# PSUM tiles, buffers and a masked copy in the second half of a two-block attention kernel

## The chip, the cores and the metric

The kernel runs on one core of one Trainium2 chip. The metric is device time in microseconds (us), the slowest core's, here the only one's. Every run is quoted by the median of its executions. "Granted clock" below is the share of full speed at which TensorE's clock was let through, and an "eviction" is a copy out of PSUM, the memory that the matmuls of this kernel write.

## The reference, cut to what matters

Two independent blocks with the same shapes (2048 tokens, width 640, 32 heads of 20) are computed and joined along the last axis. Block A is softmax attention in a sliding window of 256. Block B is linear attention:

```python
phi = lambda t: jnp.where(t > 0, t + 1, jnp.exp(t)) + 1e-6
pq, pk = phi(q), phi(k)
kv  = jnp.einsum("bhsd,bhse->bhde", pk, v)          # 20x20 state per head
z   = jnp.einsum("bhsd->bhd", pk)
num = jnp.einsum("bhqd,bhde->bhqe", pq, kv)
den = jnp.einsum("bhqd,bhd->bhq", pq, z)[..., None] + 1e-6
o   = num / den                                     # then  o @ wo
```

Both blocks end with a 640x640 output projection, called the tail here.

## The kernel before

Order of work: load A; project q, k, v of A; attention of A; then the part that the change touches. That part is, in program order: tail A; the q projection of B with phi; the k and v projections of B with phi; the state `kv_ps` (with a column of ones in v, so that it holds z too); a block-diagonal copy `kvBD` of the state; q times state and the division; tail B. A scheduler orders the instructions of each engine at build time, so work of neighbouring steps interleaves where tiles are free.

The q projection in channel-major form. One PSUM tile holds 128x2048 f32 (`P` by `NQT` times `NQ`), and B has one buffer for it:

```python
for c in range(KT):                                   # 5 channel blocks
    ps = psq.tile([P, NQT, NQ], F32, name="ps")       # psum_bufs=1 for B
    for nt in range(NQT):
        for kt in range(KT):
            nc.tensor.matmul(ps[:, nt, :], ...)       # 20 matmuls of 512 columns
    chunk = stage.tile([P, S], BF16, name="chunk")
    e = scr.tile([P, NQT, NQ], BF16, name="e")
    nc.scalar.activation(out=e[:], in_=ps[:], func=ACT.Exp)
    r = scr.tile([P, NQT, NQ], BF16, name="r")
    nc.scalar.activation(out=r[:], in_=ps[:], func=ACT.Relu)
    ...                                               # min/add on VectorE into chunk
    for h, src_row, cnt, dst_off in head_pieces(c):   # DMA rows into pq_pad[0..7]
        eng.dma_start(out=dst, in_=chunk[src_row : src_row + cnt, :])
```

The tail (both blocks; one buffer for `T2`, one for `pso`):

```python
for tb in range(NT):                                  # 16 token blocks
    T2 = pt2.tile([P, KT, P], BF16, name="T2")
    ...                                               # 5 transposes
    oT = tsb.tile([P, KT, P], BF16, name="oT_cmp")
    nc.any.tensor_copy(out=oT[:], in_=T2[:])
    pso = pto.tile([P, 1024], F32, name="pso")
    ...                                               # 10 matmuls
    osb = tsb.tile([P, D], BF16, name="osb")
    nc.any.tensor_copy(out=osb[:], in_=pso[:, 0:D])
    nc.sync.dma_start(out=out2[...], in_=osb[:])
```

The state and its block-diagonal copy, and the first use of it:

```python
nc.any.memset(kvBD[:], 0.0)
...                                                   # 8 groups x 16 matmuls into kv_ps
for hg in range(HG):
    for j in range(4):                                # 32 copies of 20x21
        nc.any.tensor_copy(
            out=kvBD[HD * j : HD * j + Dh, hg, HD * j : HD * j + HV],
            in_=kv_ps[HD * j : HD * j + Dh, hg % 2, hg // 2, HV * j : HV * j + HV],
        )
...
for tb in range(NT):
    O_ps = psn.tile([P, HG, P], F32, name="O_psB")
    for hg in range(HG):
        nc.tensor.matmul(O_ps[:, hg, :], lhsT=pq_pad[hg][:, tb * P : (tb + 1) * P],
                         rhs=kvBD[:, hg, :], start=True, stop=True)
    ...                                               # den, reciprocal, multiply -> otokB
```

The softmax here doesn't subtract the row's maximum and nothing guards it: scores larger than these inputs give would overflow.

Of the kernel before, what the change touches and what calls it, by code (L numbers as in the profile page):

```python
# [8 lines left out]
P = 128  # L9
ALU = mybir.AluOpType  # L10
ACT = mybir.ActivationFunctionType
BF16 = mybir.dt.bfloat16
F32 = mybir.dt.float32
# [3 lines left out]
def kernel(  # L17
# [40 lines left out]
    while h0 < H:  # L58
# [26 lines left out]
        base=-1,  # L85
        channel_multiplier=1,
    )
    woA_sb = const.tile([P, KT, D], BF16, name="woA_sb")
    woB_sb = const.tile([P, KT, D], BF16, name="woB_sb")
    otokA = const.tile([P, NT, D], BF16, name="otokA")  # L90
# [16 lines left out]
    dma_engines = [nc.sync, nc.scalar, nc.gpsimd]  # L107

    def proj_channel_major(
        name, xT, w, col_base, pads, mode, psum_bufs, stage_bufs, sbuf_side="right"  # L110
    ):
        with ExitStack() as stack:
            psq = stack.enter_context(
                tc.tile_pool(name=f"psq_{name}", bufs=psum_bufs, space=bass.MemoryType.PSUM, side="left")
            )
            stage = stack.enter_context(
                tc.tile_pool(name=f"stage_{name}", bufs=stage_bufs, side=sbuf_side)
            )
            scr = None
            if mode == "phi":  # L120
                scr = stack.enter_context(
                    tc.tile_pool(name=f"scr_{name}", bufs=1, side=sbuf_side)
                )
            dcount = 0
            for c in range(KT):
                ps = psq.tile([P, NQT, NQ], F32, name="ps")
                for nt in range(NQT):
                    for kt in range(KT):
                        nc.tensor.matmul(  # L129
                            ps[:, nt, :],  # L130
                            lhsT=w[:, kt, col_base + c * P : col_base + (c + 1) * P],
                            rhs=xT[:, kt, nt * NQ : (nt + 1) * NQ],
                            start=(kt == 0),
                            stop=(kt == KT - 1),
                        )
                chunk = stage.tile([P, S], BF16, name="chunk")
                cv = chunk[:].rearrange("p (n f) -> p n f", f=NQ)
                if mode == "scale":
                    nc.scalar.activation(out=cv, in_=ps[:], func=ACT.Copy, scale=scale)  # L139
                elif mode == "copy":  # L140
                    nc.any.tensor_copy(out=cv, in_=ps[:])  # L141
                elif mode == "phi":
                    e = scr.tile([P, NQT, NQ], BF16, name="e")
                    nc.scalar.activation(out=e[:], in_=ps[:], func=ACT.Exp)
                    r = scr.tile([P, NQT, NQ], BF16, name="r")
                    nc.scalar.activation(out=r[:], in_=ps[:], func=ACT.Relu)  # L146
                    nc.vector.tensor_scalar(
                        out=cv,
                        in0=e[:],
                        scalar1=1e-6,  # L150
                        scalar2=1.0 + 1e-6,
                        op0=ALU.add,
                        op1=ALU.min,
                    )
                    nc.vector.tensor_tensor(out=cv, in0=cv, in1=r[:], op=ALU.add)
                else:
                    raise ValueError(mode)
                for h, src_row, cnt, dst_off in head_pieces(c):
                    hg, j = divmod(h, 4)
                    dst = pads[hg][HD * j + dst_off : HD * j + dst_off + cnt, :]  # L160
                    eng = dma_engines[dcount % len(dma_engines)]
                    dcount += 1
                    eng.dma_start(out=dst, in_=chunk[src_row : src_row + cnt, :])

    def proj_token_major(name, xT, w, col_base, dstv_fn, mode, psum_bufs):
        with ExitStack() as stack:
# [38 lines left out]
                else:  # L205
                    raise ValueError(mode)

    def tail(name, o_tok_all, wo_sb, col0, stack, psum_side, psum_bufs):
        if True:
            pt2 = stack.enter_context(  # L210
                tc.tile_pool(name=f"pt2_{name}", bufs=psum_bufs, space=bass.MemoryType.PSUM, side=psum_side)
            )
            pto = stack.enter_context(
                tc.tile_pool(name=f"pto_{name}", bufs=psum_bufs, space=bass.MemoryType.PSUM, side=psum_side)
            )
            tsb = stack.enter_context(tc.tile_pool(name=f"tsb_{name}", bufs=2, side="right"))
            for tb in range(NT):
                T2 = pt2.tile([P, KT, P], BF16, name="T2")
                for c in range(KT):
                    nc.tensor.transpose(  # L220
                        T2[:, c, :], o_tok_all[:, tb, c * P : (c + 1) * P], ident[:]
# [4 lines that stand above are left out]
                for c in range(KT):  # L226
                    for n0 in range(0, D, NQ):
                        n1 = min(D, n0 + NQ)
                        nc.tensor.matmul(  # L229
                            pso[:, n0:n1],  # L230
                            lhsT=oT[:, c, :],
                            rhs=wo_sb[:, c, n0:n1],
                            start=(c == 0),
                            stop=(c == KT - 1),
                        )
                osb = tsb.tile([P, D], BF16, name="osb")
                nc.any.tensor_copy(out=osb[:], in_=pso[:, 0:D])  # L237
                nc.sync.dma_start(
                    out=out2[tb * P : (tb + 1) * P, col0 : col0 + D], in_=osb[:]
                )  # L240
# [11 lines left out]
    vaugA_v = vaugA[:].rearrange("p t (h e) -> p t h e", e=HV)  # L252
    nc.vector.memset(vaugA_v[:, :, :, Dh:HV], 1.0)

    proj_channel_major("qA", xTA, wA, 0, q_pad, "scale", psum_bufs=2, stage_bufs=5)
    proj_channel_major("kA", xTA, wA, D, k_pad, "copy", psum_bufs=2, stage_bufs=5)
    proj_token_major(
        "vA", xTA, wA, 2 * D, lambda tb: vaugA_v[:, tb, :, 0:Dh], "copy", psum_bufs=2
    )
# [80 lines left out]
    for g in range(HG):  # L340
# [10 lines left out]

    tstA = ExitStack()
    tail("A", otokA, woA_sb, 0, tstA, "right", 1)
    proj_channel_major(
        "pqB", xTB, wB, 0, pq_pad, "phi", psum_bufs=1, stage_bufs=4, sbuf_side="left"
    )
    tstA.close()

    with ExitStack() as stack:
        pst = stack.enter_context(  # L360
            tc.tile_pool(name="pst_kvB", bufs=2, space=bass.MemoryType.PSUM, side="left")
        )
        scrt = stack.enter_context(tc.tile_pool(name="scrt_kvB", bufs=2, side="right"))
        for tb in range(NT):
            ps = pst.tile([P, 1536], F32, name="pstkv")
            for n0 in range(0, 2 * D, NQ):
                n1 = min(2 * D, n0 + NQ)
# [26 lines left out]

    kvsb = ctx.enter_context(tc.tile_pool(name="kvsb", bufs=1, side="right"))
    kvBD = kvsb.tile([P, HG, P], BF16, name="kvBD")
    nc.any.memset(kvBD[:], 0.0)
    with ExitStack() as kvs:
        kvp = kvs.enter_context(tc.tile_pool(name="kvp", bufs=1, space=bass.MemoryType.PSUM, side="left"))
        kv_ps = kvp.tile([P, 2, 4, P], F32, name="kv_ps")  # L400
        for hg in range(HG):
            for tb in range(NT):
                nc.tensor.matmul(  # L403
                    kv_ps[:, hg % 2, hg // 2, 0 : 4 * HV],
                    lhsT=pk_pad[:, tb, hg * P : (hg + 1) * P],
                    rhs=vaugB[:, tb, hg * 4 * HV : (hg + 1) * 4 * HV],
                    start=(tb == 0),
                    stop=(tb == NT - 1),
                )
        for hg in range(HG):  # L410
            for j in range(4):
                nc.any.tensor_copy(  # L412
                    out=kvBD[HD * j : HD * j + Dh, hg, HD * j : HD * j + HV],
                    in_=kv_ps[HD * j : HD * j + Dh, hg % 2, hg // 2, HV * j : HV * j + HV],
                )
    stB2.close()

    persB3 = ctx.enter_context(tc.tile_pool(name="persB3", bufs=1, side="left"))
    otokB = persB3.tile([P, NT, D], BF16, name="otokB")
    with ExitStack() as nms:  # L420
        psn = nms.enter_context(tc.tile_pool(name="psn", bufs=2, space=bass.MemoryType.PSUM, side="left"))
        nrmB = nms.enter_context(tc.tile_pool(name="nrmB", bufs=2, side="left"))
        for tb in range(NT):
            O_ps = psn.tile([P, HG, P], F32, name="O_psB")
            for hg in range(HG):
                nc.tensor.matmul(  # L426
                    O_ps[:, hg, :],
                    lhsT=pq_pad[hg][:, tb * P : (tb + 1) * P],
                    rhs=kvBD[:, hg, :],
                    start=True,  # L430
                    stop=True,
                )
            ov = O_ps[:].rearrange("p g (j e) -> p g j e", e=HD)
            den = nrmB.tile([P, HG, 4, 1], F32, name="denB")
            nc.vector.tensor_scalar_add(out=den[:], in0=ov[:, :, :, Dh : Dh + 1], scalar1=1e-6)  # L435
            recip = nrmB.tile([P, HG, 4, 1], F32, name="recipB")
# [5 lines left out]
                in1=recip[:].to_broadcast([P, HG, 4, Dh]),  # L442
                op=ALU.mult,
            )
        tail("B", otokB, woB_sb, D, nms, "right", 1)


# [28 lines left out]
```

## Time and profile before

465.16 us, median of 6 runs (463.51 to 466.59).

| stretch before, us | what | TensorE busy | what the rest is |
|---|---|---|---|
| 0 to 286.7 | block A up to its attention | 246.3 | not touched by the change |
| 286.7 to 336.5 | tail A with part of the q projection of B | 44.0 of 49.8 | waits for evictions |
| 336.5 to 353.6 | rest of the q projection of B | 9.5 of 17.1 | two waits for Exp and Relu |
| 353.6 to 397.1 | k and v projections of B | 43.2 of 43.5 | dense |
| 397.1 to 412.5 | state and its copies | 6.6 of 15.4 | TensorE waits |
| 412.5 to 438.4 | q times state, division, half of tail B | 24.0 of 25.9 | VectorE 22.0 |
| 438.4 to 463.9 | nine blocks of tail B | 15.9 of 25.5 | waits for copies |

The table by windows of the profile before. The columns after the window and its length are busy time (with the number of instructions) of the engines, the mean granted TensorE clock, the share of the DMA engines and GB/s:

```profile
core 0: us, PE busy (x) PEld busy (x) DVE busy (x) ACT busy (x) POOL busy (x), PEclk, DMA share, GB/s
286.70:336.50 49.80, 44.04 (x302) 23.11 (x307) 23.31 (x32) 21.24 (x22) 8.72 (x8) 0.97 0.27 78
336.50:353.60 17.10, 9.52 (x31) 3.57 (x31) 2.63 (x4) 7.98 (x5) 0.99 (x2) 0.80 0.18 53
353.60:397.06 43.46, 43.16 (x235) 23.38 (x239) 13.53 (x31) 29.91 (x45) 1.51 (x3) 1.00 0.05 13
397.06:412.50 15.44, 6.58 (x129) 6.56 (x129) 0.91 (x2) 7.43 (x35) 0.95 (x1) 0.80 0.01 2
412.50:438.40 25.90, 24.00 (x234) 16.62 (x238) 21.96 (x54) 5.36 (x8) 0.00 (x0) 0.86 0.12 39
438.40:463.90 25.50, 15.91 (x128) 9.12 (x130) 3.98 (x9) 7.00 (x11) 0.00 (x0) 1.00 0.19 65
```

From 412.5 to 438.4 the profile shows TensorE 24.00 us at matmuls and 16.62 us at weight loads in 25.90 us, so the two overlap, and it shows the ends of matmuls as modelled; 24.0 of 25.9 therefore does not show that matmuls bound that stretch. What does is seen instruction by instruction. The timeline of the kernel before (start, duration, engine, line, operation, output and inputs, count; in brackets the idle time of the engine before it and what ended it), first around the q projection of B:

```profile
338.89 1.88 ACT L144 ACTIVATE e<-ps 128x2048 bf16<-128x2048 f32 x1 [0.39 <-PE ps L129]
340.67 1.87 ACT L146 ACTIVATE r<-ps 128x2048 bf16<-128x2048 f32 x1
342.59 7.21 PE L129 MATMUL ps<-xT_inB,w_inB 128*128 128x512 bf16 x20 [3.73 <-ACT r L146]
353.60 6.65 PE L369 MATMUL pstkv<-w_inB,xT_inB 128*128 128x512 bf16 x34 [3.79 <-ACT r L146]
```

One PSUM tile, one buffer: TensorE stands 3.73 us until Exp and Relu have read it. The twenty matmuls behind it take 7.21 us, 0.36 us each, where packed matmuls of this shape, such as the ten before the wait, start 0.216 us apart. The granted clock was 0.50 from 342.6 to 347.

Next, the timeline around the state:

```profile
399.14 6.56 PE L403 MATMUL kv_ps<-vaugB,pk_pad 128*128 128x84 bf16 x128 [2.11 <-ACT vaugB L392]
405.81 6.42 ACT L412 CAST kvBD<-kv_ps 20x21 bf16<-20x21 f32 x32 [6.72 <-PE kv_ps L403]
412.48 2.81 PE L426 MATMUL O_psB<-kvBD,pq_pad 128*128 128x128 bf16 x16 [6.79 <-ACT kvBD L412]
```

Thirty-two tiny copies take 6.42 us of ScalarE in a row, 0.20 us each for 420 numbers, and TensorE waits 6.79 us for them. And in the last stretch, two steps of tail B:

```profile
443.54 0.49 DVE L224 COPY oT_cmp<-T 128x640 bf16<-128x640 bf16 x1 [1.97 <-PE T L220]
444.09 1.53 PE L229 MATMUL pso<-woB_sb,oT_cmp 128*128 128x512 bf16 x9 [0.65 <-DVE oT_cmp L224]
446.49 1.53 PE L229 MATMUL pso<-woB_sb,oT_cmp 128*128 128x512 bf16 x10 [0.58 <-DVE oT_cmp L224]
```

Each block of 2.40 us has a hole near 0.6 us in which TensorE waits for its transposed input to be copied out of the only transpose buffer.

### The profile page before, as it was taken

Reading aid. Unit: us, or ns where it says so; the run is one execution under the profiler, and the core shown is the slowest. Engines: PE = TensorE matmul, PEld = TensorE weight load, DVE = VectorE, ACT = ScalarE, POOL = GpSimd, SP = SyncE. Lnnn points to the kernel's source line nnn. Section 1 sums busy time; section 2 is a strip of 40 time slices with the busy share of each in tenths; the row PEclk is TensorE's granted clock in tenths of the full one; section 3 lists DMA queues with packets and bytes.
Section 4 is the critical chain, followed back from the end, with each engine's and each line's share of the span. In section 5 each row is a group of like instructions: output and inputs, shape, how many; then the busy total and the mean of one; then the engine's idle time right before and its main releaser. Section 6 shows DMA issues by size and latency. Waiting matters only on the chain. (4 is left out here: it accounts for less than half of the span.)

```text
span 463.9 us, 10081 instructions
## 1 busy us (share of the span) xinstructions
PE 389.5 (84%) x4291; PEld 225.8 (49%) x4316; DVE 195.0 (42%) x497; ACT 274.7 (59%) x322; POOL 25.8 (6%) x48
## 2 busy tenths in 40 slices
PE   0498979889999999999999999889866999739875
PEld 0143435455555555655555555445423555626642
DVE  0000251066656665565665656624412332128721
ACT  1034103589888899899888886651435777342222
POOL 1013120000000000000000002200101000000000
PEclk9999999965555555555555555999979999868999
DMA  8954341095000000000000000033321000001111
GB/s 178 316 152 120 95 127 47 12 232 199 3 1 1 4 2 1 3 1 1 4 2 1 3 1 1 30 95 111 96 76 52 1 0 1 1 1 44 58 62 66
DMA packets 34361, 25.56 MB, mean 55 GB/s; under 512 B 23180, under 2 KB 32396, under 8 KB 34316
## 3 DMA queue, kind: packets, MB, share of 16 engines
q1 hardware_dynamic: 31628, 19.65, 15.0%
q0 software_dynamic: 1632, 2.61, 2.4%
q10 hardware_dynamic: 1056, 2.66, 2.3%
q8 instruction: 34, 0.56, 0.5%
q14 instruction: 11, 0.09, 0.1%
HBM read 6.55 MB, written 5.24 MB: 25 GB/s over the span
## 5 line engine op out<-in xcount | busy, mean ns | idle before, releaser
L297 ACT ACTIVATE p<-S_ps 128x1152 bf16<-128x1152 f32 (+3 forms) x176 | 173.5, 1041 | 20.4 <-PE S_ps L288 16.2
L288 PE MATMUL S_ps<-q_pad,k_pad 20*128 20x128 bf16 x1440 | 117.1, 289 | 15.6 <-ACT p L297 13.7
L317 PE MATMUL O_qb<-vaugA,p 128*128 128x21 bf16 x1440 | 96.1, 185 | 1.7 <-DVE p L307 0.9
L317 PEld LDWEIGHTS <-p 128*128 128x128 bf16 x1440 | 64.4, 106 | 55.9 <-DVE p L301 26.9
L301 DVE TENSOR_TENSOR p<-p,maskE 128x384 bf16<-128x384 bf16 (+1 forms) x154 | 53.9, 350 | 57.8 <-ACT p L297 56.8
L307 DVE TENSOR_TENSOR p<-p,maskD 128x384 bf16<-128x384 bf16 (+1 forms) x176 | 60.6, 345 | 24.8 <-ACT p L297 24.2
L129 PE MATMUL ps<-xT_inA,w_inA 128*128 128x512 bf16 x196 | 45.8, 397 | 20.3 <-DMA w_inA<-in_A_wqkv_dram 18.0
L288 PEld LDWEIGHTS <-k_pad 20*128 20x128 bf16 x1440 | 46.4, 104 | 29.4 <-issue 18.8
L237 ACT CAST osb<-pso 128x640 bf16<-128x640 f32 x25 | 17.4, 694 | 51.8 <-PE pso L229 39.1
L369 PE MATMUL pstkv<-w_inB,xT_inB 128*128 128x512 bf16 (+1 forms) x235 | 43.2, 343 | 4.1 <-ACT r L146 3.8
L129 PEld LDWEIGHTS <-w_inA 128*128 128x128 bf16 x200 | 20.2, 101 | 45.7 <-DMA w_inA<-in_A_wqkv_dram 18.0
L229 PEld LDWEIGHTS <-oT_cmp 128*128 128x128 bf16 x320 | 24.1, 98 | 34.9 <-DVE oT_cmp L224 12.0
L369 PEld LDWEIGHTS <-xT_inB 128*128 128x128 bf16 x240 | 23.5, 98 | 24.0 <-issue 3.6
L141 DVE CAST chunk<-ps 128x2048 bf16<-128x2048 f32 x4 | 9.2, 2291 | 56.3 <-PE ps L129 54.3
L129 PE MATMUL ps<-xT_inB,w_inB 128*128 128x512 bf16 x96 | 28.7, 437 | 4.1 <-ACT r L146 3.7
L229 PE MATMUL pso<-woB_sb,oT_cmp 128*128 128x128 bf16 (+1 forms) x154 | 25.5, 301 | 6.7 <-DVE oT_cmp L224 4.7
L139 ACT ACTIVATE chunk<-ps 128x2048 bf16<-128x2048 f32 x5 | 9.4, 1877 | 33.1 <-PE ps L129 30.7
L229 PE MATMUL pso<-woA_sb,oT_cmp 128*128 128x128 bf16 (+1 forms) x157 | 24.3, 298 | 5.4 <-ACT oT_cmp L224 2.9
L190 ACT CAST vaugA<-pst 128x640 bf16<-128x640 f32 x14 | 9.7, 695 | 29.1 <-PE pst L180 29.1
L180 PE MATMUL pst<-w_inA,xT_inA 128*128 128x128 bf16 (+1 forms) x157 | 21.7, 297 | 2.8 <-DVE chunk L141 2.6
L224 DVE COPY oT_cmp<-T 128x640 bf16<-128x640 bf16 x22 | 10.7, 489 | 20.5 <-PE T L220 20.3
L378 ACT ACTIVATE et<-pstkv 128x640 bf16<-128x640 f32 x16 | 11.3, 704 | 13.1 <-PE pstkv L369 13.1
(47 smaller groups left out, 243.8 us busy)
## 6 DMA issues: line engine op xcount, KB each, us to landing
out_dram<-osb SPq DMA_DIRECT2D x32, 160.0 KB
w_inA<-in_A_wqkv_dram SPq DMA_DIRECT2D x3, 800.0 KB
w_inB<-in_B_wqkv_dram SPq DMA_DIRECT2D x3, 800.0 KB
woA_sb<-in_A_wo_dram SPq DMA_DIRECT2D x1, 800.0 KB
woB_sb<-in_B_wo_dram SPq DMA_DIRECT2D x1, 800.0 KB
q_pad<-chunk SPq DMA_DIRECT2D x10, 80.0 KB
q_pad<-chunk POOLq DMA_DIRECT2D x10, 80.0 KB, 3.6
k_pad<-chunk SPq DMA_DIRECT2D x10, 80.0 KB
```

The source lines that it names most:

```text
L129: nc.tensor.matmul(ps[:, nt, :], lhsT=w[:, kt, col_base + c * P : col_base + (c + 1) * P], rhs=xT[:, kt, nt * NQ : (nt + 1) * NQ], start=( ...
L180: nc.tensor.matmul(ps[:, n0:n1], lhsT=xT[:, kt, tb * P : (tb + 1) * P], rhs=w[:, kt, col_base + n0 : col_base + n1], start=(kt == 0), stop ...
L224: nc.any.tensor_copy(out=oT[:], in_=T2[:])
L229: nc.tensor.matmul(pso[:, n0:n1], lhsT=oT[:, c, :], rhs=wo_sb[:, c, n0:n1], start=(c == 0), stop=(c == KT - 1),)
L237: nc.any.tensor_copy(out=osb[:], in_=pso[:, 0:D])
L288: nc.tensor.matmul(S_ps[:, i, kbi, :], lhsT=k_pad[hg][HD * j : HD * j + Dh, kb * P : (kb + 1) * P], rhs=q_pad[hg][HD * j : HD * j + Dh, qb ...
L297: nc.scalar.activation(out=p[:, 0:nh, 0:nkb, :], in_=S_ps[:, 0:nh, 0:nkb, :], func=ACT.Exp)
L301: nc.vector.tensor_tensor(out=p[:, 0:nh, 0, :], in0=p[:, 0:nh, 0, :], in1=maskE[:, None, :].to_broadcast([P, nh, P]), op=ALU.mult,)
L307: nc.vector.tensor_tensor(out=p[:, 0:nh, nkb - 1, :], in0=p[:, 0:nh, nkb - 1, :], in1=maskD[:, None, :].to_broadcast([P, nh, P]), op=ALU.mult,
L317: nc.tensor.matmul(O_qb[:, oslot(h), 0:HV], lhsT=p[:, i, kbi, :], rhs=vaugA[:, kb, h * HV : (h + 1) * HV], start=(kbi == 0), stop=(kbi == ...
L369: nc.tensor.matmul(ps[:, n0:n1], lhsT=xTB[:, kt, tb * P : (tb + 1) * P], rhs=wB[:, kt, D + n0 : D + n1], start=(kt == 0), stop=(kt == KT - 1),
L378: nc.scalar.activation(out=e[:], in_=kv_view, func=ACT.Exp)
```

## The change

The intent: take the waits for single PSUM buffers and for the small copies out of the second half. Three parts, independent in the code; the q and k projections of A get only a new calling form.

1. The 32 copies become one multiply by a 0/1 mask on VectorE; the matmuls of q times state take 84 columns instead of 128 (the 128 matmuls that make the state had 84 before, too).
2. The q projection of B uses PSUM tiles of half the size (128x1024 f32, one buffer), and the first five of the 16 k/v blocks are written before tail A and q projection release their pools, with one buffer, so that they can interleave with both.
3. The last nine blocks of tail B get two `T2` and three `pso` buffers; result tiles go from two to three buffers.

```diff
+    BDmask = const.tile([P, 4 * HV], BF16, name="BDmask")      # ones in the four 20x21 blocks
 ...
-            for c in range(KT):
-                ps = psq.tile([P, NQT, NQ], F32, name="ps")
+        for c in range(KT):
+            chunk = stage.tile([P, S], BF16, name="chunk")
+            for sp in range(nsplit):
+                ps = psq.tile([P, nqg, NQ], F32, name="ps")
 ...
     proj_channel_major(
-        "pqB", xTB, wB, 0, pq_pad, "phi", psum_bufs=1, stage_bufs=4, sbuf_side="left"
+        "pqB", xTB, wB, 0, pq_pad, "phi", stpq, psum_bufs=1, stage_bufs=4, nsplit=2,
+        sbuf_side="left",
     )
-    tstA.close()
-            tc.tile_pool(name="pst_kvB", bufs=2, space=bass.MemoryType.PSUM, side="left")
+            tc.tile_pool(name="pst_kvB", bufs=1, space=bass.MemoryType.PSUM, side="left")
-        for tb in range(NT):
+        for tb in range(5):
 ...
+    stpq.close()
+    tstA.close()
+            tc.tile_pool(name="pst_kvB2", bufs=2, ..., reuse_waits="tile")
+        for tb in range(5, NT):                                # the same body
 ...
-        for hg in range(HG):
-            for j in range(4):
-                nc.any.tensor_copy(...)
+        nc.vector.tensor_tensor(
+            out=kvBD[:].rearrange("p (k par) f -> p k par f", par=2)[:, :, :, 0 : 4 * HV],
+            in0=kv_ps[:].rearrange("p par k f -> p k par f")[:, :, :, 0 : 4 * HV],
+            in1=BDmask[:, None, None, :].to_broadcast([P, HG // 2, 2, 4 * HV]),
+            op=ALU.mult,
+        )
 ...
-                    O_ps[:, hg, :],
+                    O_ps[:, hg, 0 : 4 * HV],
-        tail("B", otokB, woB_sb, D, nms, "right", 1)
+        tail("B", otokB, woB_sb, D, nms, "right", 1, tbs=range(7), tsb=tsbB)
+    with ExitStack() as nms2:
+        tail("B2", otokB, woB_sb, D, nms2, "right", 2, tbs=range(7, NT), pso_bufs=3, tsb=tsbB)
```

(`reuse_waits="tile"` lets a new pool's tile wait for the tiles it overlaps instead of for the whole old pool; the tails' PSUM pools have it too.)

More of the change, by code (lines that the diff above doesn't have):

```diff
@@ L87 @@
     )
+    BDmask = const.tile([P, 4 * HV], BF16, name="BDmask")
+    nc.vector.memset(BDmask[:], 0.0)
+    for j in range(4):
+        nc.vector.memset(BDmask[HD * j : HD * j + Dh, HV * j : HV * j + HV], 1.0)
     woA_sb = const.tile([P, KT, D], BF16, name="woA_sb")
@@ L109, in proj_channel_major @@
     def proj_channel_major(
-        name, xT, w, col_base, pads, mode, psum_bufs, stage_bufs, sbuf_side="right"
-    ):
-        with ExitStack() as stack:
-            psq = stack.enter_context(
-                tc.tile_pool(name=f"psq_{name}", bufs=psum_bufs, space=bass.MemoryType.PSUM, side="left")
-            )
-            stage = stack.enter_context(
-                tc.tile_pool(name=f"stage_{name}", bufs=stage_bufs, side=sbuf_side)
-            )
-            scr = None
-            if mode == "phi":
-                scr = stack.enter_context(
-                    tc.tile_pool(name=f"scr_{name}", bufs=1, side=sbuf_side)
-                )
-            dcount = 0
-            for c in range(KT):
-                ps = psq.tile([P, NQT, NQ], F32, name="ps")
-                for nt in range(NQT):
+        name, xT, w, col_base, pads, mode, stack, psum_bufs, stage_bufs,
+        nsplit=1, sbuf_side="right",
+    ):
+        nsplit = max(1, min(nsplit, NQT))
+        nqg = NQT // nsplit
+        psq = stack.enter_context(
+            tc.tile_pool(name=f"psq_{name}", bufs=psum_bufs, space=bass.MemoryType.PSUM, side="left")
+        )
+        stage = stack.enter_context(
+            tc.tile_pool(name=f"stage_{name}", bufs=stage_bufs, side=sbuf_side)
+        )
+        scr = None
+        if mode == "phi":
+            scr = stack.enter_context(tc.tile_pool(name=f"scr_{name}", bufs=1, side=sbuf_side))
+        dcount = 0
+        for c in range(KT):
+            chunk = stage.tile([P, S], BF16, name="chunk")
+            for sp in range(nsplit):
+                ps = psq.tile([P, nqg, NQ], F32, name="ps")
+                for g in range(nqg):
+                    nt = sp * nqg + g
                     for kt in range(KT):
                         nc.tensor.matmul(
-                            ps[:, nt, :],
+                            ps[:, g, :],
                             lhsT=w[:, kt, col_base + c * P : col_base + (c + 1) * P],
@@ L135, in proj_channel_major @@
                         )
-                chunk = stage.tile([P, S], BF16, name="chunk")
-                cv = chunk[:].rearrange("p (n f) -> p n f", f=NQ)
+                cv = chunk[:, sp * nqg * NQ : (sp + 1) * nqg * NQ].rearrange(
+                    "p (n f) -> p n f", f=NQ
+                )
                 if mode == "scale":
@@ L142, in proj_channel_major @@
                 elif mode == "phi":
-                    e = scr.tile([P, NQT, NQ], BF16, name="e")
+                    e = scr.tile([P, nqg, NQ], BF16, name="e")
                     nc.scalar.activation(out=e[:], in_=ps[:], func=ACT.Exp)
-                    r = scr.tile([P, NQT, NQ], BF16, name="r")
+                    r = scr.tile([P, nqg, NQ], BF16, name="r")
                     nc.scalar.activation(out=r[:], in_=ps[:], func=ACT.Relu)
@@ L157, in proj_channel_major @@
                     raise ValueError(mode)
-                for h, src_row, cnt, dst_off in head_pieces(c):
-                    hg, j = divmod(h, 4)
-                    dst = pads[hg][HD * j + dst_off : HD * j + dst_off + cnt, :]
-                    eng = dma_engines[dcount % len(dma_engines)]
-                    dcount += 1
-                    eng.dma_start(out=dst, in_=chunk[src_row : src_row + cnt, :])
+            for h, src_row, cnt, dst_off in head_pieces(c):
+                hg, j = divmod(h, 4)
+                dst = pads[hg][HD * j + dst_off : HD * j + dst_off + cnt, :]
+                eng = dma_engines[dcount % len(dma_engines)]
+                dcount += 1
+                eng.dma_start(out=dst, in_=chunk[src_row : src_row + cnt, :])
     def proj_token_major(name, xT, w, col_base, dstv_fn, mode, psum_bufs):
@@ L206, in proj_token_major, with tail @@
                     raise ValueError(mode)
-    def tail(name, o_tok_all, wo_sb, col0, stack, psum_side, psum_bufs):
+    def tail(name, o_tok_all, wo_sb, col0, stack, psum_side, psum_bufs, tbs=range(NT), pso_bufs=1, tsb=None):
         if True:
             pt2 = stack.enter_context(
-                tc.tile_pool(name=f"pt2_{name}", bufs=psum_bufs, space=bass.MemoryType.PSUM, side=psum_side)
+                tc.tile_pool(name=f"pt2_{name}", bufs=psum_bufs, space=bass.MemoryType.PSUM, side=psum_side, reuse_waits="tile")
             )
             pto = stack.enter_context(
-                tc.tile_pool(name=f"pto_{name}", bufs=psum_bufs, space=bass.MemoryType.PSUM, side=psum_side)
+                tc.tile_pool(name=f"pto_{name}", bufs=pso_bufs, space=bass.MemoryType.PSUM, side=psum_side, reuse_waits="tile")
             )
-            tsb = stack.enter_context(tc.tile_pool(name=f"tsb_{name}", bufs=2, side="right"))
-            for tb in range(NT):
+            tsb = tsb or stack.enter_context(tc.tile_pool(name=f"tsb_{name}", bufs=2, side="right"))
+            for tb in tbs:
                 T2 = pt2.tile([P, KT, P], BF16, name="T2")
@@ L253 @@
     nc.vector.memset(vaugA_v[:, :, :, Dh:HV], 1.0)
-    proj_channel_major("qA", xTA, wA, 0, q_pad, "scale", psum_bufs=2, stage_bufs=5)
-    proj_channel_major("kA", xTA, wA, D, k_pad, "copy", psum_bufs=2, stage_bufs=5)
+    st = ExitStack()
+    proj_channel_major("qA", xTA, wA, 0, q_pad, "scale", st, psum_bufs=2, stage_bufs=5)
+    st.close()
+    st = ExitStack()
+    proj_channel_major("kA", xTA, wA, D, k_pad, "copy", st, psum_bufs=2, stage_bufs=5)
+    st.close()
     proj_token_major(
@@ L353 @@
     tail("A", otokA, woA_sb, 0, tstA, "right", 1)
+    stpq = ExitStack()
     proj_channel_major(
-        "pqB", xTB, wB, 0, pq_pad, "phi", psum_bufs=1, stage_bufs=4, sbuf_side="left"
-    )
+        "pqB", xTB, wB, 0, pq_pad, "phi", stpq, psum_bufs=1, stage_bufs=4, nsplit=2,
+        sbuf_side="left",
+    )
+    with ExitStack() as stack:
+        pst = stack.enter_context(
+            tc.tile_pool(name="pst_kvB", bufs=1, space=bass.MemoryType.PSUM, side="left")
+        )
+        scrt = stack.enter_context(tc.tile_pool(name="scrt_kvB", bufs=2, side="right"))
+        for tb in range(5):
+            ps = pst.tile([P, 1536], F32, name="pstkv")
+            for n0 in range(0, 2 * D, NQ):
+                n1 = min(2 * D, n0 + NQ)
+                for kt in range(KT):
+                    nc.tensor.matmul(
+                        ps[:, n0:n1],
+                        lhsT=xTB[:, kt, tb * P : (tb + 1) * P],
+                        rhs=wB[:, kt, D + n0 : D + n1],
+                        start=(kt == 0),
+                        stop=(kt == KT - 1),
+                    )
+            kv_view = ps[:, 0:D].rearrange("p (h d) -> p h d", d=Dh)
+            e = scrt.tile([P, H, Dh], BF16, name="et")
+            nc.scalar.activation(out=e[:], in_=kv_view, func=ACT.Exp)
+            r = scrt.tile([P, H, Dh], BF16, name="rt")
+            nc.scalar.activation(out=r[:], in_=kv_view, func=ACT.Relu)
+            pkv = pk_pad_v[:, tb, :, 0:Dh]
+            nc.vector.tensor_scalar(
+                out=pkv,
+                in0=e[:],
+                scalar1=1e-6,
+                scalar2=1.0 + 1e-6,
+                op0=ALU.add,
+                op1=ALU.min,
+            )
+            nc.vector.tensor_tensor(out=pkv, in0=pkv, in1=r[:], op=ALU.add)
+            vv_view = ps[:, D : 2 * D].rearrange("p (h d) -> p h d", d=Dh)
+            nc.any.tensor_copy(out=vaugB_v[:, tb, :, 0:Dh], in_=vv_view)
+    stpq.close()
     tstA.close()
@@ L360 @@
         pst = stack.enter_context(
-            tc.tile_pool(name="pst_kvB", bufs=2, space=bass.MemoryType.PSUM, side="left")
-        )
-        scrt = stack.enter_context(tc.tile_pool(name="scrt_kvB", bufs=2, side="right"))
-        for tb in range(NT):
+            tc.tile_pool(name="pst_kvB2", bufs=2, space=bass.MemoryType.PSUM, side="left",
+                         reuse_waits="tile")
+        )
+        scrt = stack.enter_context(tc.tile_pool(name="scrt_kvB2", bufs=2, side="right"))
+        for tb in range(5, NT):
             ps = pst.tile([P, 1536], F32, name="pstkv")
@@ L396 @@
     kvBD = kvsb.tile([P, HG, P], BF16, name="kvBD")
-    nc.any.memset(kvBD[:], 0.0)
     with ExitStack() as kvs:
@@ L409 @@
                 )
-        for hg in range(HG):
-            for j in range(4):
-                nc.any.tensor_copy(
-                    out=kvBD[HD * j : HD * j + Dh, hg, HD * j : HD * j + HV],
-                    in_=kv_ps[HD * j : HD * j + Dh, hg % 2, hg // 2, HV * j : HV * j + HV],
-                )
+        nc.vector.tensor_tensor(
[3 more added lines that the diff above has]
+            op=ALU.mult,
+        )
     stB2.close()
@@ L419 @@
     otokB = persB3.tile([P, NT, D], BF16, name="otokB")
+    tsbB = ctx.enter_context(tc.tile_pool(name="tsb_B", bufs=3, side="right"))
     with ExitStack() as nms:
@@ L426 @@
                 nc.tensor.matmul(
-                    O_ps[:, hg, :],
+                    O_ps[:, hg, 0 : 4 * HV],
                     lhsT=pq_pad[hg][:, tb * P : (tb + 1) * P],
-                    rhs=kvBD[:, hg, :],
+                    rhs=kvBD[:, hg, 0 : 4 * HV],
                     start=True,
@@ L432 @@
                 )
-            ov = O_ps[:].rearrange("p g (j e) -> p g j e", e=HD)
+            ov = O_ps[:, :, 0 : 4 * HV].rearrange("p g (j e) -> p g j e", e=HV)
             den = nrmB.tile([P, HG, 4, 1], F32, name="denB")
```

## The prediction

> **What bounds the kernel now.** The projections and attention of A run to 286.7 us of the 463.9 us span. The order of instructions on every engine is the same there in both kernels, so this part should not move. Only the last 177.2 us can. Three stretches lie there (table by windows, timeline, chain of waits):
>
> - 286.7 to 397.1: A's output projection (tail A), B's q projection with phi, B's k/v projection. TensorE needs about 90 us (16 tail blocks of 1.64, 100 matmuls of 0.2135, 16 k/v blocks of 2.67, all read from packed pieces of the timeline), so some 20 us are waits or half clock. Before, tail A costs 2.8 us a block, because the 0.49 to 0.82 us evictions stand between its transposes and matmuls; the q projection twice waits 3.7 us for its own 1.88 us Exp and Relu; the matmuls after the first of these waits are granted 0.50. The k/v stage (353.6 to 397.1) is dense: 43.1 us of 44.
> - 397.1 to 412.5: kv state, 6.6 us of matmuls after a 2.1 us wait, then 32 copies of 20x21 on ScalarE, 0.20 us apart, 6.4 us, with TensorE idle 6.8 us; the clock then stays at 0.50 until 419.5.
> - 412.5 to 463.9: normalisation, bound by VectorE (22 of 26 us), then nine tail blocks at 2.40 us where TensorE waits 0.6 to 0.8 us for each copy (one buffer each).
>
> [...]
>
> **What the change does.**
>
> 1. 32 copies become one VectorE multiply by a mask, 128x672 from PSUM; I estimate 0.86 us from the 0.82 us of the 128x640 multiply. TensorE's gap falls from 6.8 to about 1.2 us: saves 5.6. [...]the first normalisation starts faster: saves 2.7. Narrower state matmuls (84 for 128 columns) and the lost memset are off the path.
> 2. The last nine tail blocks get 2 transpose and 3 projection buffers; the order becomes 10 transposes, 20 matmuls. A pair then takes about 3.8 us instead of 4.8 (2.7 + 0.57 + a remaining hole near 0.5): saves about 4.2.
> 3. The q projection goes to half-size PSUM tiles, so five k/v blocks interleave with it and tail A. Exp and Relu of 128x1024 take an estimated 1.02 us each (between 0.70 for 640 and 1.88 for 2048). Some 15 us of k/v work moves into holes, but tail A stays at 2.7 to 2.9 us a block, since its buffers remain single and ScalarE gets more work between its copies; after tail A the q and k/v tiles, single-buffered, alternate with waits of 1 to 2 us each (my walk by hand: 22 us for 17 us of TensorE work), and the join to the last eleven k/v blocks waits about 2 us. Net: saves about 7 (range 2 to 15).
>
> Sum: 5.6 + 2.7 + 4.2 + 7 = 19.5 us, all on the critical path. Predicted 445.5 us, 438 to 453. Faster by over 2% 0.95, within 2% 0.04, slower 0.01.
>
> **Right or wrong would show as:** attention unmoved to 286.7; one masked multiply near 0.86 us with a TensorE gap under 1.5 us and full clock after it; last tail blocks near 1.9 us; end of the k/v matmuls near 390.
>
> **What would make it wrong:** ScalarE's static order in the interleaved part, stalling tail A or dropping the clock (less gain), or denser packing there than I walked (more); output DMAs holding the three result buffers; a slow strided mask multiply.

What no trace or run of this case shows is cut from the prediction, and the cuts are marked. The sum, 5.6 + 2.7 + 4.2 + 7 = 19.5 us, stands, but the term of 2.7 us has lost the reason given for it, a statement about the clock after a short gap that was not shown.

## The result, and the profile after

The changed kernel takes 448.83 us (median of 8 runs, 446.29 to 449.5), against 465.86 us for the kernel before in the same rounds. The ratio is 0.9628, with a 95% interval of 0.9605 to 0.9651. Ratios in this document are the mean time of one kernel's runs over that of the kernel before's runs of the same rounds, so they are not quite the ratio of the medians quoted. A gain quoted from a ratio is one minus it, times the 465 us before.

The table by windows of the changed kernel, cut at the same events:

```profile
286.70:336.00 49.30, 46.90 (x323) 24.80 (x328) 23.27 (x37) 25.67 (x35) 7.20 (x5) 0.98 0.23 73
336.00:359.00 23.00, 17.40 (x84) 8.16 (x85) 8.00 (x17) 15.46 (x19) 2.50 (x5) 1.00 0.20 53
359.00:388.90 29.90, 29.69 (x162) 15.98 (x164) 8.83 (x21) 19.95 (x31) 1.50 (x3) 1.00 0.07 19
388.90:398.50 9.60, 6.56 (x128) 6.55 (x129) 1.68 (x3) 1.98 (x3) 0.00 (x0) 0.82 0.01 2
398.50:424.40 25.90, 22.08 (x229) 14.71 (x233) 21.30 (x54) 5.37 (x8) 0.00 (x0) 0.87 0.12 39
424.40:446.40 22.00, 15.49 (x133) 9.37 (x134) 2.49 (x6) 8.87 (x14) 0.00 (x0) 0.98 0.22 76
```

The two profiles side by side, with the events read from the timelines (the last attention matmul of A starts at 286.5 in both):

| from, to | before | after | difference | predicted |
|---|---|---|---|---|
| last attention matmul, end of the k/v matmuls | 110.6 | 102.4 | -8.2 | -7 |
| then to the first matmul with the state copy | 15.4 | 9.7 | -5.7 | -5.6 |
| then to the end of the last division | 26.0 | 25.9 | -0.1 | -2.7 |
| then to the end | 25.5 | 22.0 | -3.5 | -4.2 |
| sum | 177.4 | 159.9 | -17.5 | -19.5 |

The third row is the surprise. The timeline around the state after the change:

```profile
390.96 6.56 PE L451 MATMUL kv_ps<-vaugB,pk_pad 128*128 128x84 bf16 x128 [2.11 <-ACT vaugB L441]
397.63 0.86 DVE L458 TENSOR_TENSOR kvBD<-kv_ps,BDmask 128x672 bf16<-128x672 f32 x1 [6.92 <-PE kv_ps L451]
398.54 2.15 PE L475 MATMUL O_psB<-kvBD,pq_pad 128*128 128x84 bf16 x16 [1.02 <-DVE kvBD L458]
```

The masked multiply takes 0.86 us, as estimated, and the gap falls from 6.79 to 1.02 us. But the first sixteen matmuls still take 2.15 us (2.81 before, with 128 columns); their predecessors of the same 84 columns run at 0.05 us each (128 in 6.56 us). The granted clock during these sixteen, and after them:

```profile
398.50:401.50 3.00, 1.88 (x16) 0.97 (x15) 0.98 (x4) 0.00 (x0) 0.00 (x0) 0.98 0.00 0
401.50:408.00 6.50, 5.42 (x47) 4.15 (x49) 4.15 (x10) 1.20 (x2) 0.00 (x0) 0.50 0.00 0
```

So the slow start is not a matter of the clock: it is granted at 0.98 while they crawl, and falls to 0.50 only afterwards. The single records of the two traces say the same: the first eight matmuls start 0.21 to 0.29 us apart here, and 0.23 to 0.30 us apart in the kernel before, where the clock was 0.50. Only the second eight follow the clock (and the columns): 0.04 us apart here, 0.11 before. The weight loads in between show idle time with no releaser ("issue" means that the profile sees nothing that the engine waits for):

```profile
398.72 0.56 PEld L475 LDWEIGHTS <-pq_pad 128*128 128x128 bf16 x3 [1.30 <-issue]
399.47 1.09 PEld L475 LDWEIGHTS <-pq_pad 128*128 128x128 bf16 x12 [0.19 <-issue]
```

And the last stretch:

```profile
428.56 0.72 PE L228 MATMUL T<-ident,otokB 128*128 128x128 bf16 x10
429.04 0.49 DVE L232 COPY oT_cmp<-T 128x640 bf16<-128x640 bf16 x1 [3.18 <-PE T L228]
429.59 2.89 PE L237 MATMUL pso<-woB_sb,oT_cmp 128*128 128x512 bf16 x19 [0.31 <-DVE oT_cmp L232]
433.35 2.89 PE L237 MATMUL pso<-woB_sb,oT_cmp 128*128 128x512 bf16 x20 [0.30 <-DVE oT_cmp L232]
```

A pair of blocks takes 3.76 us instead of 4.80; one hole of 0.3 us per pair is left (0.6 in the fourth pair, which takes 4.05).

### The profile page after: what moved, and what is told of

The parts are those of the page before. It is cut to its first block, busy times and chain, and to the rows that moved or that the text cites. A ratio compares the mean times of both kernels' runs of the same rounds, so it can differ in the third digit from the quotient of the medians.

```text
span 446.4 us, 10067 instructions
## 1 busy us (share of the span) xinstructions
PE 383.2 (86%) x4291; PEld 222.6 (50%) x4316; DVE 194.5 (44%) x508; ACT 273.1 (61%) x305; POOL 24.9 (6%) x47
## 4 chain that ended last, share of the span: by engine, by line
PE 50%; ACT 32%; DVE 6%; issue 4%; DMA 3%; SPq 3%; ACTq 1%; another core or an unknown queue 0%; DVEq 0%
ACT p L309 27%; PE ps L136 12%; PE S_ps L300 9%; PE pso L237 7%; PE pstkv L418 7%; PE O_qb L329 6%; PE pst L188 5%; SPq L102 3%; DVE otokB L488 2%; PE pstkv L381 2%; DMA w_inA<-in_A_wqkv_dram 2%; PE kv_ps L451 1%; PE T L228 1%; ACT r L154 1%; DMA out_dram<-osb 1%
## 5 line engine op out<-in xcount | busy, mean ns | idle before, releaser
L136 PE MATMUL ps<-xT_inA,w_inA 128*128 128x512 bf16 x196 | 44.5, 388 | 21.7 <-DMA w_inA<-in_A_wqkv_dram 19.4
L418 PE MATMUL pstkv<-w_inB,xT_inB 128*128 128x512 bf16 (+1 forms) x162 | 29.7, 343 | 2.2 <-ACT r L154 2.0
L136 PE MATMUL ps<-xT_inB,w_inB 128*128 128x512 bf16 x98 | 25.9, 393 | 3.7 <-ACT r L154 3.3
L418 PEld LDWEIGHTS <-xT_inB 128*128 128x128 bf16 x165 | 16.1, 98 | 16.0 <-issue 1.9
L232 ACT COPY oT_cmp<-T 128x640 bf16<-128x640 bf16 x16 | 11.2, 698 | 15.7 <-PE T L228 15.4
L152 ACT ACTIVATE e<-ps 128x1024 bf16<-128x1024 f32 x10 | 10.3, 1027 | 13.7 <-PE ps L136 9.3
```

The source lines that it names most:

```text
L136: nc.tensor.matmul(ps[:, g, :], lhsT=w[:, kt, col_base + c * P : col_base + (c + 1) * P], rhs=xT[:, kt, nt * NQ : (nt + 1) * NQ], start=(k ...
L418: nc.tensor.matmul(ps[:, n0:n1], lhsT=xTB[:, kt, tb * P : (tb + 1) * P], rhs=wB[:, kt, D + n0 : D + n1], start=(kt == 0), stop=(kt == KT - 1),
```

## The experiments

Eleven runs were made, all with correct results. The first four (e1 to e4) isolate parts, e5 to e8 test the slow start, and e9 to e11, with e4, the buffers of the q projection.

### Does each part earn what its stretch shows? (e1, e2, e3)

e1 is the kernel before plus part 1 alone: the `BDmask` tile, the masked multiply, 84 columns. e2 is the kernel before plus part 3 alone. e3 is the kernel before plus part 2 alone.

```diff
# e1, against the kernel before
-                nc.any.tensor_copy(out=kvBD[...], in_=kv_ps[...])        # x32
+        nc.vector.tensor_tensor(out=kvBD..., in0=kv_ps..., in1=BDmask..., op=ALU.mult)
# e2, against the kernel before
-        tail("B", otokB, woB_sb, D, nms, "right", 1)
+        tail("B", ..., tbs=range(7), tsb=tsbB)
+        tail("B2", ..., 2, tbs=range(7, NT), pso_bufs=3, tsb=tsbB)
# e3, against the changed kernel: parts 1 and 3 taken back (its tail pools keep reuse_waits)
```

> The kernel before with one part of the change alone: the 32 block copies of the kv state become the one masked multiply (with the 84-column state matmuls that go with it). Main theory, from the two traces: the TensorE gap falls from 6.8 to 1.0 us and nothing else moves, because the first pass over the q tiles stays slow for another reason than the clock: gain 5.5 to 6 us, and the span from the first state matmul to the last normalisation stays near 26 us. Rival (the one of the prediction): a shorter gap also brings the clock back to full, gain 8 to 8.5 us and that span near 23.5 us.

> The kernel before with the last nine tail blocks in 2 transpose and 3 projection buffers, nothing else. Main theory: a pair of blocks takes 3.75 us instead of 4.8 us; gain 3 to 4 us. Rival: the gain of the whole change in this stretch came from the result buffers or from the earlier start, then the gain here is under 1 us.

> The kernel before with only the half-size q projection tiles and the five interleaved k/v blocks. If the three parts add up as the two traces say, the k/v matmuls end 8.2 us earlier and the gain is 7.5 to 8.5 us. Rival: the parts overlap, and the three single gains sum to clearly more or less than the 17 us of the whole change.

Measured, beside 465.86 us before in the same rounds: e1 459.19 us, ratio 0.9861 (0.9811 to 0.9911), a gain of 6.5 us; e2 463.42 us, 0.9936 (0.9897 to 0.9975), 3.0 us; e3 458.49 us, 0.9845 (0.9811 to 0.9879), 7.2 us. The sum is 16.7 us, against 17.1 us for the whole (ratio 0.9633 in a repeat, e5). Each is a gain of under 2%, but none of the intervals reaches 1. The parts add within the noise, which by these intervals is some 3 us on the sum. In e2 the last stretch falls from 25.5 to 22.0 us, exactly as in the whole change, so it is not an earlier start. e2 has the third result buffer too; but in the profile before no engine waits for an output DMA in that stretch, so it was the PSUM buffers that held it.

e1 does not settle its own question. From the first matmul with the state copy to the end of the last division it shows 24.7 us, between the 26 of one theory and the 23.5 of the other. The unaltered changed kernel shows 25.9 us in one profile and 24.8 us in another (e5): the half clock after the slow start lasted 6.8 us in the first and 3.4 us in the second. Another experiment was needed.

### Why did the first division not start earlier? (e5 to e8)

The build's own list of instructions names a suspect. Each q tile was filled by four or five DMAs on different queues, and the first time TensorE loads one as weights, that load carries a wait for every one of them. All had landed some 30 us earlier (in the changed kernel the last was issued at 360.9 us, the longest time to landing shown is 4.7 us, and the first of these loads starts at 397.3 us):

```
Ldweights pq_pad 0 [waits DMAHW1,DMAHW2,DMAHW0,DMASW0]
Matmult O_psB<-kvBD,pq_pad 0 128x84 [waits DVE]
Ldweights pq_pad 1 [waits DMAHW4,DMAHW3,DMAHW5,DMASW2,DMASW1]
Matmult O_psB<-kvBD,pq_pad 1 128x84
...
```

(Names shortened, and all waits before a load written on it: in the build two EventSemaphore instructions stand before each of these loads with three or four of its waits, and the load itself has one.) That is 36 waits on eight loads, and sixteen EventSemaphore instructions. The first eight matmuls start 0.21 to 0.29 us apart, and the eight that follow, without these waits, run packed, 0.04 us apart, though they load columns of the same q tiles that TensorE has not read before.

All three test kernels add matmuls whose result is never read to the changed kernel, before the state matmuls, where TensorE stands 2.11 us for the last k/v eviction. These read k/v block 14, so that they do not wait for that eviction; the four that e8 adds after the state matmuls read block 15:

```diff
         kv_ps = kvp.tile([P, 2, 4, P], F32, name="kv_ps")
+        dummy = wrm.tile([P, NQ], F32, name="dummy")       # a tile of its own
# e6: 8 tiny ones, each with another q tile as weights
+        for hg in range(HG):
+            nc.tensor.matmul(dummy[:, 0:32], lhsT=pq_pad[hg][:, 0:P],
+                             rhs=vaugB[:, NT - 2, 0:32], start=True, stop=True)
# e7: instead, 9 long ones on weights that waited long ago
+        for i in range(9):
+            nc.tensor.matmul(dummy[:, 0:512], lhsT=woB_sb[:, 0, 0:P],
+                             rhs=vaugB[:, NT - 2, 0:512], start=True, stop=True)
# e8: the 8 of e6 with 512 columns, and after the state matmuls
+        for i in range(4):
+            nc.tensor.matmul(dummy[:], lhsT=woB_sb[:, 0, 0:P],
+                             rhs=vaugB[:, NT - 1, 0:NQ], start=True, stop=True)
```

> The changed kernel unaltered, as the reference on this chip for the next three: about 449 us, ratio to the kernel before 0.963.

> The changed kernel plus eight tiny matmuls (32 columns, result never read) that load each q tile once while TensorE waits 2.1 us for the last k/v eviction, so that the waits on the DMA semaphores of the q tiles are passed there. Theory A: the slow first pass over the q tiles (16 state matmuls in 2.15 us though the granted clock was 1.00) is the 36 semaphore waits on its eight weight loads; then the 16 take about 1 us, the first normalisation starts about 1 us earlier, gain 0.8 to 2.5 us (more if the clock then stays up). Theory B: it is the clock or the first use of the state tile; then nothing moves, gain under 0.3 us.

> The changed kernel plus nine dummy matmuls of 512 columns in the same 2.1 us hole, on weights whose data has long landed, so that [...]the semaphore waits stay where they were. If the half clock of 3.3 us during the kv state matmuls comes from this hole, they take near 4.9 us instead of 6.6 and the gain is 1 to 2 us; the first 16 state matmuls still take about 2 us under theory A. Under theory B they get faster too.

> The changed kernel plus both: eight dummy matmuls of 512 columns on the q tiles in the first hole and four on other weights in the 1.0 us hole before the state matmuls. If both causes are real and independent, the gains add: kv state matmuls near 4 to 5 us, the 16 state matmuls near 1 us, no half clock in the first normalisations, gain 3 to 6 us over the changed kernel. Risk: the dummies overrun the holes and give part of it back.

| run | median us | ratio to before (95%) | 128 state matmuls | first 16 with the copy | first of these to last division |
|---|---|---|---|---|---|
| e5, the changed kernel again | 448.27 | 0.9633 (0.9606 to 0.9660) | 6.56 us | 2.19 us | 24.8 us |
| e6, q tiles touched early | 445.59 | 0.9583 (0.9556 to 0.9610) | 6.56 us | 0.76 us | 22.2 us |
| e7, hole filled, waits left | 446.90 | 0.9602 (0.9575 to 0.9630) | 4.98 us | 2.48 us | 25.4 us |
| e8, both | 443.74 | 0.9539 (0.9513 to 0.9564) | 4.98 us | 0.77 us | 22.2 us |

The timeline of e6, matmuls only:

```profile
389.89 1.44 PE L454 MATMUL dummy<-vaugB,pq_pad 128*128 128x32 bf16 x8
392.17 6.56 PE L460 MATMUL kv_ps<-vaugB,pk_pad 128*128 128x84 bf16 x128 [0.84 <-ACT vaugB L441]
399.75 0.76 PE L484 MATMUL O_psB<-kvBD,pq_pad 128*128 128x84 bf16 x16 [1.02 <-DVE kvBD L467]
```

The eight touches now take 1.44 us, in time that TensorE had free, and the sixteen matmuls fall from 2.15 to 0.76 us. e6 has all 36 waits on the eight touches and none on the sixteen, and e7 has them where they were. Theory A holds: the waits, all long satisfied, cost about 1.4 us on the critical path (the sixteen take 2.19 us in e5, 0.76 us in e6). By division that is some 0.04 us a wait, or 0.09 us for each of the sixteen EventSemaphore instructions, an estimate from these two runs. e7 is the control: there the hole is filled too, but without touching the q tiles, and the sixteen stay slow:

```profile
399.10 2.48 PE L484 MATMUL O_psB<-kvBD,pq_pad 128*128 128x84 bf16 x16 [1.02 <-DVE kvBD L467]
```

Its first eight start 0.21 to 0.32 us apart, as in the changed kernel; it is longer than 2.15 us because the clock fell within the sixteen, at 400.6 (the mean over 399.0 to 402.0 is 0.76).

The clock, in the 3 us from the first of these sixteen matmuls and the 3.6 us after, by windows (length, TensorE busy, clock, DMA), for e5:

```profile
399.40:402.40 3.00, 1.89 (x16) 1.00 0.00 0
402.40:406.00 3.60, 2.56 (x25) 0.60 0.00 0
```

and for e6:

```profile
399.70:402.70 3.00, 1.52 (x29) 1.00 0.00 0
402.70:406.30 3.60, 3.10 (x40) 1.00 0.00 0
```

In all four profiles of kernels with the masked multiply and no early touch (the changed kernel twice, e1, e7) the clock falls to 0.50 after the slow start or, in e7, during it (means of 0.50, 0.60, 0.56 and 0.50 over the 3.6 us that follow the first 3); in all four with it (e6, e8, e10, e11) it stays at 1.00. So in these eight the half clock came with the slow start, four times of four, and in none of the four without it. Why it follows the thinner stream (16 against 29 matmuls in 3 us) is not shown. Together the two are worth 2.6 us of that stretch against e5 (24.8 to 22.2), 3.7 us against the first profile. In time, every run of e6 (445.43 to 447.0 us) is faster than every run of e5 (447.39 to 448.91), while the intervals of the two ratios just touch.

e7 shows the other hole. By windows, the 128 state matmuls of e5 and then, in a fence of its own, those of e7:

```profile
391.90:398.40 6.50, 6.50 (x128) 0.74 0.01 3
```

```profile
393.10:398.10 5.00, 4.98 (x128) 1.00 0.01 3
```

With TensorE kept busy through the 2.1 us hole the clock stays at 1.00 in all four kernels that do it (e7, e8, e10, e11), and the state takes 4.98 instead of 6.56 us. But the hole alone does not decide. In e9, reported below, nothing fills it, and the state takes 4.98 us all the same; the seven other profiles that leave a hole of 2.11 us there (before, after, e1 to e5) show 6.56 us. In the profiles before and after, the clock is 0.50 or 1.00 (a stretch with another mean holds a step), and all 16 steps lie whole multiples of 3.41 us apart (in the changed kernel at 391.13, 394.54, 401.37 and 408.19 us). By stretches cut at such multiples, TensorE only: the one before the fall at 391.13 in the changed kernel, then, in a fence of its own, the two that share the hole in e9:

```profile
387.71:391.13 3.42, 1.31 (x13) 1.00 0.00 0
```

```profile
407.10:410.52 3.42, 2.96 (x18) 1.00 0.00 0
410.52:413.93 3.41, 1.75 (x47) 1.00 0.00 0
```

In the changed kernel one stretch holds the whole hole, TensorE is busy for 1.31 of 3.42 us, and the clock falls at its end; in e9 two stretches share the hole and the clock holds. The waits of the q projection before the change look alike: the first lay mostly in one stretch (0.93 us busy of 3.41) and was followed by 6.83 us at 0.50, the second was shared by two (1.64 and 1.40 us busy) and the clock stayed at 1.00. No rule is shown by this: the fall at 401.37 came after a stretch with 1.88 us busy of 3.42. The steps begin elsewhere in each run (at 23.90 us before, at 22.49 us after), so whether an unfilled hole of this length was followed by half clock, in seven profiles of eight, may be partly luck.

The nine dummies of e7 fitted the hole: its state matmuls start 2.12 us after the last k/v matmul, 2.11 us in e5. They saved 1.6 us there, of which 0.7 us was lost again in the division (25.4 against 24.8 us), where the half clock lasted longer (6.8 against 3.4 us); and in its profile the k/v matmuls, which no dummy precedes, ended 0.7 us later after attention. The ratio of e7 overlaps that of e5: in time alone it is unclear. e8 has both; the gains add, and it is clear of the changed kernel (1.0%: 0.9539 over 0.9633).

### What did the q projection gain from: moved work or buffers? (e4, e9)

Part 2 does two things at once. e4 keeps the half-size tiles, gives them two buffers (together the size of the one large tile), and moves no k/v block. e9 is e4 with one buffer.

```diff
# e4, against the kernel before
-        "pqB", ..., psum_bufs=1, stage_bufs=4, sbuf_side="left"
+        "pqB", ..., psum_bufs=2, stage_bufs=4, nsplit=2, sbuf_side="left",
# e9, against e4
-        "pqB", ..., psum_bufs=2, ...
+        "pqB", ..., psum_bufs=1, ...
```

> The kernel before with the q projection in half-size PSUM tiles, two buffers, and no k/v block moved forward. Theory of the prediction: k/v work moved into the holes of tail A is what earns the 8.2 us, then this kernel gains clearly less, 2 to 5 us. Rival: the gain is the removal of the two 3.7 us waits and of the 7 us at half clock after them, for which smaller tiles and a second buffer are enough, then this kernel gains 7 to 9 us, as much as the interleaved one.

> As the run with half-size q projection tiles, but one PSUM buffer instead of two, no k/v block moved. Theory: what earns there is that the matmuls of one tile overlap Exp and Relu of the other, so with one buffer each of the 1.02 us activations is waited for again and, with no k/v work to put there, fifty matmuls left after tail A take near 4.4 us per ten: gain 0 to 2 us or a small loss against the kernel before. Rival: the smaller tile is enough because each wait shrinks from 3.7 to about 2 us and the clock stays up: gain 5 us or more.

e4: 457.88 us, ratio 0.9830 (0.9801 to 0.9859), a gain of 7.9 us, as much as e3 with its moved blocks (7.2 us) within the intervals. From the last attention matmul to the end of the k/v matmuls it needs 102.6 us, the changed kernel 102.4. The rival was right. The timeline of e4 after tail A, matmuls only:

```profile
336.04 6.45 PE L132 MATMUL ps<-xT_inB,w_inB 128*128 128x512 bf16 x29
345.96 29.36 PE L380 MATMUL pstkv<-w_inB,xT_inB 128*128 128x512 bf16 x160 [3.47 <-ACT r L150]
```

One wait is left, at the end, 3.47 us; the tiles before it overlap with the Exp and Relu of the other buffer. The same place in e9:

```profile
337.85 2.32 PE L132 MATMUL ps<-xT_inB,w_inB 128*128 128x512 bf16 x10
342.19 4.00 PE L132 MATMUL ps<-xT_inB,w_inB 128*128 128x512 bf16 x10 [2.03 <-ACT r L150]
348.29 3.68 PE L132 MATMUL ps<-xT_inB,w_inB 128*128 128x512 bf16 x10 [2.09 <-ACT r L150]
353.99 2.32 PE L132 MATMUL ps<-xT_inB,w_inB 128*128 128x512 bf16 x10 [2.02 <-ACT r L150]
```

e9: 477.06 us, ratio 1.0229 (1.0199 to 1.0259), 10.6 us slower than before, worse than either theory said. After tail A there are five waits of 2.0 to 2.6 us instead of two of 3.7, since fifty of the hundred matmuls are left then, against thirty before. Three of the five are followed by half clock (ten matmuls in 3.68 or 4.00 instead of 2.32 us); the mean clock over 337.9 to 365.0 is 0.81. So the smaller tile by itself is a loss. In the changed kernel the k/v blocks fill most of these waits (three of 1.5 to 2.0 us are left); in e4 the second buffer does. Either is enough, and neither was measured to be better than the other.

### Versions that beat both (e10, e11)

e10 is e8 with the q projection of e4 in place of the moved blocks, 34 lines less. e11 adds a second buffer for the transposes of tail A; PSUM had room for it there, as e11 built and ran.

```diff
# e10, against e8: the five k/v blocks go back into the one loop of sixteen
-        "pqB", ..., psum_bufs=1, stage_bufs=4, nsplit=2,
+        "pqB", ..., psum_bufs=2, stage_bufs=4, nsplit=2,
# e11, against e10
-    tail("A", otokA, woA_sb, 0, tstA, "right", 1)
+    tail("A", otokA, woA_sb, 0, tstA, "right", 2)
```

> Masked multiply, split tail, dummies on the q tiles and before the state matmuls, but with the two-buffer q projection in place of the interleaved k/v blocks. If the interleaving adds nothing over a second buffer, this is as fast as the same kernel with the interleaving: 443 to 445 us, ratio 0.952 to 0.956. If the interleaving earns by itself, it is 446 us or more.

> The kernel of the run before this one, with a second transpose buffer for tail A[...]. If the single transpose buffer is what holds tail A at 2.8 us a block, the blocks fall towards 2.2 to 2.5 us and the gain is 2 to 5 us more. If ScalarE's static order of evictions holds it, nothing moves: under 1 us.

e10: 444.71 us, ratio 0.9543 (0.9525 to 0.9562), the same as e8 (0.9539). e11: 442.63 us, 0.9501 (0.9475 to 0.9527), the fastest of all. By the medians it gains 2.1 us, the low end of what was expected of it; that the second transpose buffer earns this is not shown. In the two profiles the part after attention takes the same: from the last attention matmul to the end 155.3 us in e10 and 155.4 us in e11, and to the end of the k/v matmuls 103.1 and 103.2. Tail A does end earlier in e11 (46.2 us after the last attention matmul, against 49.9), but the q projection then has more left to do. What differs between the profiles is the untouched part before: its last matmul starts at 288.1 and 286.5. That start varies between 286.5 and 288.2 over the profiles of this study, with the same instructions, so gains near 1 us are better read from the traces than from medians.

## Why the prediction was right or wrong

The time was right: 448.83 us, in the range of 438 to 453, 3.3 us above the middle. In part that was luck: a term of 2.7 us failed, the q projection gave 1.2 us more than its middle, and the range was 15 us wide. Taken point by point:

- **Attention does not move.** Right: the last attention matmul starts at 286.5 us in both profiles.
- **The masked multiply near 0.86 us, and a gap near 1.2 us instead of 6.8.** Right: 0.86 and 1.02 us; 5.7 us saved where 5.6 were predicted.
- **"the first normalisation starts faster: saves 2.7."** Wrong, and this is the step that failed: that stretch went from 26.0 to 25.9 us (24.8 in the second profile, e5), and the full clock that was to follow the multiply gave way to 0.50. The slow start before the change had been put down to the half clock, which was indeed granted there, 0.50; that it was the cause was the author's estimate. After the change the clock was 0.98 and the first eight matmuls started as far apart as before. What held them was the waits for DMA semaphores on the first load of each q tile (e6: the sixteen go from 2.15 to 0.76 us), and where the start was slow the half clock came back (four profiles of four). With these waits moved, 2.6 us did appear, close to the 2.7 predicted for another reason.
- **Tail B: a pair in 3.8 us, saving 4.2.** The mechanism and the pair were right (3.75 to 4.05 us); the saving was 3.5. From the first to the last projection matmul the nine blocks save 4.1 us, but the start costs 0.6 us more than before, as the first transposes of the new pools wait 0.82 us for the last eviction from the old one, and the sum did not contain that.
- **The q projection and the k/v blocks: net 7 (2 to 15).** The size was right, 8.2, and so was the detail: tail A stays as long as before (49.3 against 49.8 us), the alternating part takes 23 us (predicted 22 and a join of 2), the k/v matmuls end at 388.9 (predicted 390). The reason given, k/v work moved into holes, was incomplete: e4 gains the same with no work moved. What counts is that TensorE has something to do while a q tile is read; that may be other work or the next buffer. Without either, the half-size tile costs 10.6 us (e9), a risk that the prediction did not name.

## What to carry to other kernels

Splitting a PSUM tile without adding a buffer or other work can add more waits than it shortens (five of 2.0 to 2.6 us for two of 3.7 here), so count what TensorE can do while the tile is read before making it smaller. A low granted clock beside slow matmuls does not prove that the clock is the cause: look at the first instruction that uses tiles filled by many DMAs, and let the engine touch those tiles once in a hole it has anyway (2.15 to 0.76 us for sixteen matmuls here). A few discarded matmuls in holes of 1 and 2 us passed such waits and went with a clock of 1.00 in e8, e10 and e11, worth 1.0% in e8. That is for holes which they fit; dummies longer than their hole were not tried.
